# Retention and two MLPs on one core: two rings of PSUM banks, another order of the first units, and the first weights fetched by quarters

## The chip, the core and the metric

The kernel runs on one core of one Trainium2 chip. The metric is the device time of one execution, in microseconds (us). A core has five engines that run side by side, each taking its own instructions in a fixed order: TensorE (PE: matmuls and transposes), VectorE (DVE), ScalarE (ACT), GpSimd (POOL) and SyncE (SP), which here issues nearly all DMAs. They wait for each other through semaphores. TensorE writes its results to PSUM, a small memory of eight banks, from which ACT and DVE fetch them; a bank can be written again only when its readers are done.

## The reference

The inputs are q, k, v of shape (2, 8, 768, 64) (batches, heads, tokens, width), a decay `lam` for each head, and four weight matrices. The first part is retention:

```python
for b in range(nb):                                   # blocks of 64 tokens
    intra = (qb @ kb.T * Dmask) @ vb                  # Dmask[i, j] = lam ** (i - j) where i >= j
    inter = (qb * lam_pow) @ kv_state
    out[:, :, sl] = intra + inter
    kv_state = lam_block * kv_state + (kb * rev_pow).T @ vb
```

Its output, laid out as x of 1536 tokens x 512, goes through two MLPs, each x -> f(x @ w_in) @ w_out with a hidden width of 2048: f is relu squared in the first and max(0.01 h, h) in the second. The weights come as 64-bit floats; the rest is fp32.

## The kernel before

**Retention.** A chunk is 128 tokens (the decay makes the sum independent of the chunk's size). There are 12 units: 2 batches of 6 chunks, each with all 8 heads as 4 pairs. Called `unit n` below, each has these steps:

- `load(n, "kq")`, `load(n, "v")` (L66): 256 KB each, issued by SP into buffers that rotate (five for k, three for q, three for v).
- `transposes(n)` (L279): four transposes of k and four of q on PE, each group into its own PSUM bank; ACT copies them out (L283) as kT and qT. For a chunk with a state before it POOL then scales qT to qS (L289).
- `scores(n)` (L296): the products of kT and qT into two banks, one for the even and one for the odd heads. `mask(n)` (L301): DVE multiplies each bank by the table of decays DTr and writes Pm, which frees the bank.
- `state(n)`: POOL makes kd, the decayed k (L314), and, beyond the first chunk, tmp, the decayed old state (L327). PE multiplies kd with v (L320). DVE writes the new state (L332, or L334 for a batch's first chunk). The last chunk of a batch (units 5 and 11) has none.
- `output(n)`: per pair, state times qS (L345, not for a batch's first chunk, units 0 and 6) and v times Pm (L347). `split` takes the bank away: ACT writes the high part xhi (L69), and after it DVE the low part xlo (L70). xhi and xlo are the MLPs' input.

The order of SP and PE is that of the program; the orders of ACT, DVE and POOL are made by a scheduler, except that steps marked with `keep_in_program_order` keep theirs. `warm` (L205) is PE work without a use, transposes of the identity matrix; there are 15 of them at the start and 7 within `transposes(0)`.

**PSUM.** All tiles of PSUM, in retention and later, come from one pool of eight banks used in turn (`bank`, L59). A new tile takes the bank of the eighth tile before it and waits until that one's readers are done.

**Weights.** A matrix is fetched in pieces of 1 MB (`fetch`, L92; called p0, p1, p2, ... in their order) into two buffers `raw`, each a single DMA: p0 at the loop's i = 1, p1 at i = 9, p2 right after retention. `converting` (L99) turns a piece into fp32 in `hb` and splits it into a high and a low part: ACT L111, four steps of DVE (L112, L113, L115, L118), ACT L132 (w1h or w2h), DVE L134 (w1l or w2l). Each call of `convert` sets off one more of these DVE steps for each piece in work. In retention this happens at i = 3 to 7, so that p0 is whole by the MLPs' first matmul; p1 and p2 are converted at its end and after it. Once the MLPs have begun, the fourth DVE step of a piece, with which its `raw` buffer comes free, also fetches the next piece.

**MLPs.** They need fp32, so each product is three matmuls of high and low parts, all on L525; pairs of token tiles go through a scheme of seven products. Their instructions on PE are in the program's order too. Each of the first steps of the MLPs uses p0 (its low part from the third matmul on), then p1 about 17 us later.

Of the kernel before, what the change touches and what calls it, by code (L numbers as in the profile page):

```python
# [2 lines left out]

# [13 lines left out]
P = 128  # L17
# [3 lines left out]
def tile_retention_then_two_mlps(  # L21
# [32 lines left out]
    raw = ctx.enter_context(tc.tile_pool(name="raw", bufs=2))  # L54
    fp = ctx.enter_context(tc.tile_pool(name="fp", bufs=9))
    cv = ctx.enter_context(tc.tile_pool(name="cv", bufs=1))
    psum = ctx.enter_context(tc.tile_pool(name="psum", bufs=8, space=bass.MemoryType.PSUM))

    def bank():  # L59
        return psum.tile([P, 512], F32, tag="ps", name="ps")  # L60

    def plain():
        return fp.tile([P, TT], F32, tag="f", name="f")
# [1 line left out]
    def dma(dst, src):  # L65
        return nc.sync.dma_start(dst, src)  # L66
# [22 lines left out]
    fetched, at_work = [], []  # L89
    wts, sums, opened = {}, {}, set()  # L90

    def fetch():  # L92
        if todo:
            key = todo.pop(0)
            r = raw.tile([P, 4 * CW], I64, tag="raw", name="raw")
            k = 4 if key[2] == 0 else 2
            dma(r.rearrange("p (k f) -> p k f", k=k), source(*key))
            fetched.append((key, r))

    def converting():  # L100
        key, r = fetched.pop(0)
        l, s, n, h = key
        k = 4 if n == 0 else 2
        words = r.bitcast(U32).rearrange("p (f t) -> p f t", t=2)
        w_lo, w_hi = words[:, :, 0], words[:, :, 1]
        ve = nc.vector
        hb = cv.tile([P, 4 * CW], U32, tag="hb", name="hb", bufs=2)
        hf = hb.bitcast(F32)
        half = hb.bitcast(U16).rearrange("p (f t) -> p f t", t=2)[:, :, 0]

        nc.scalar.activation(hf, w_hi.bitcast(F32), AF.Abs)  # L111
        yield ve.tensor_scalar(out=hf, in0=hf, scalar1=2.0 ** -15, scalar2=122368.0, op0=ALU.max, op1=ALU.min)  # L112
        yield ve.tensor_scalar(out=hb, in0=hb, scalar1=3, scalar2=0x3FFFFFFF,  # L113
                               op0=ALU.logical_shift_left, op1=ALU.bitwise_and)
        yield ve.scalar_tensor_tensor(out=hb, in0=w_hi, scalar=0xC0000000, in1=hb,  # L115
                                      op0=ALU.bitwise_and, op1=ALU.bitwise_or)

        step = ve.scalar_tensor_tensor(out=half, in0=w_lo, scalar=2.0 ** -29, in1=half, op0=ALU.mult, op1=ALU.add)  # L118
        if begun_mlp:
            fetch()  # L120
        yield step
        if (l, s) != stages[0] and n == 0:
            w = hf.rearrange("p (k f) -> p k f", k=k)
            blocks = {(i, j): w[:, 2 * j:2 * j + 2, i * P:(i + 1) * P] for i in range(2) for j in range(2)}
            rb = cv.tile([P, 4 * CW], U32, tag="rb", name="rb")
            yield from weight_sums(key, f"sw{h}", blocks, rb.bitcast(F32))
        while key not in opened:
            yield None
        tags = (f"w1h{h}", f"w1l{h}") if n == 0 else ("w2h", "w2l")
        bufs = 1 if n == 0 else 3  # L130
        hi, lo = (wp.tile([P, 4 * CW], F32R, tag=tag, name=tag, bufs=bufs) for tag in tags)
        nc.scalar.copy(hi, hf)  # L132
        wts[key] = [x.rearrange("p (k f) -> p k f", k=k) for x in (hi, lo)]
        yield ve.tensor_tensor(out=lo, in0=hf, in1=hi, op=ALU.subtract)  # L134
        if (l, s) == stages[-1] and n == 1:
            while ("sums", l, s) not in opened:
                yield None
            rb = cv.tile([P, 4 * CW], U32, tag="rb", name="rb")
            w = hf.rearrange("p (k i m f) -> p k i m f", k=2, i=2, m=2)
            blocks = {(i, j): w[:, j, i] for i in range(2) for j in range(2)}  # L140
            yield from weight_sums(key, f"t{h + 2}", blocks, rb.bitcast(F32))
# [14 lines left out]
                tc.keep_in_program_order(step)  # L156


    begun_mlp = []
    opened.update(order[:5])  # L160

    xhi = [None] * NTILE
# [4 lines left out]
        xlo[t] = xp.tile([P, KD, TT], F32R, tag=f"xlo{t}", name=f"xlo{t}")  # L167

    def retention(ctx_att, att):
        nat = {  # L170
            name: ctx_att.enter_context(tc.tile_pool(name="nat" + name, bufs=n))
            for name, n in (("k", 5), ("q", 3), ("v", 3))
# [25 lines left out]
        make_identity(nc, ident)  # L198


        idle = bank()

        def warm(n):
            for _ in range(n):
                tc.keep_in_program_order(nc.tensor.transpose(idle[:, 0:P], ident, ident))  # L205

# [66 lines left out]
        def transposes(i, names="kq"):  # L273
            for name in names:
                dst = {"k": kT, "q": qT}[name]
                ps = bank().rearrange("p (a s) -> p a s", a=NP)
                src = nats[i, name]
                for p in range(NP):
                    nc.tensor.transpose(ps[:, p, :], src[:, 2 * p:2 * p + 2, :].rearrange("s h d -> s (h d)"), ident)  # L279
                if i == 0:  # L280
                    warm(3 if name == "k" else 4)
                dst[i] = tr.tile([P, NP, C], F32, tag=name, name=name + "T", bufs=2)
                nc.scalar.copy(dst[i], ps)  # L283
            return ps

        def scale_q(i, ps):
            if units[i][1]:
                qS[i] = tr.tile([P, NP, C], F32, tag="qS", name="qS")
                nc.gpsimd.tensor_tensor(out=qS[i], in0=qT[i], in1=LR, op=ALU.mult)  # L289

        def scores(i):
            raw_scores[i] = [bank().rearrange("p (a s) -> p a s", a=NP) for _ in range(2)]
            for p in range(NP):
                for par in range(2):
                    r = slice(par * D, (par + 1) * D)
                    nc.tensor.matmul(raw_scores[i][par][:, p, :], kT[i][r, p, :], qT[i][r, p, :], start=True, stop=True)  # L296

        def mask(i):
            Pm[i] = wk.tile([P, 2, NP, C], F32, tag="Pm", name="Pm")
            for par in range(2):  # L300
                ve.tensor_tensor(out=Pm[i][:, par], in0=raw_scores[i][par], in1=DT[:, par], op=ALU.mult)  # L301
# [65 lines left out]
        scale_q(1, q1)  # L367
        scores(1)
        state(0)
        mask(0)  # L370
        output(0)
        scale_q(2, transposes(2))
        state(1)
        mask(1)
        scores(2)
        for i in range(n_units):
            if i and i + 2 < n_units:
                scale_q(i + 2, transposes(i + 2))
            if i + 4 < n_units:
                load(i + 4, "kq")  # L380
            if i + 2 < n_units:
                load(i + 2, "v")
            if i in (1, 9):
                fetch()
            if i:
                if i > 1:
                    state(i)
                output(i)
                if i + 1 < n_units:
                    mask(i + 1)  # L390
                if i + 2 < n_units:
                    scores(i + 2)
            if 3 <= i <= 7:
                convert(pin=True)


    with ExitStack() as ctx_att:
        att = ctx_att.enter_context(tc.tile_pool(name="att", bufs=1))
        with tc.manual_schedule(engines={mybir.EngineType.SP, mybir.EngineType.PE}):
            retention(ctx_att, att)  # L400


    late = ctx.enter_context(tc.tile_pool(name="late", bufs=1, reuse_waits="tile"))
    spill = [[[dram.tile([P, DM], F32, name=f"spill{l}{t}{m}") for m in range(4)] for t in range(NTILE)]
# [387 lines left out]
            return parts + [first(l, s, 2)] + [second_last(s, t) for t in range(NTILE)]  # L792
        return parts + [second(l, s, 0), first(l, s, 2), second(l, s, 1), second(l, s, 2)]

    begun_mlp.append(True)
    fetch()
    opened.update(order[:7])
    with tc.manual_schedule(engines={mybir.EngineType.PE}):
        for l, s in stages:
# [29 lines left out]
```

## Time and profile before

| | us |
|---|---|
| median of 3 runs (lowest, highest) | 574.09 (573.87, 574.21) |
| the profiled execution | 573.56 |
| its span, from the first instruction to the last | 571.6 |
| PE busy | 561.2 (98% of the span) |
| DVE busy | 407.6 (71%) |
| ACT busy | 304.6 (53%) |
| PE's waits: L525 for DVE g0l L467 | 3.0, 3 times |
| PE's waits: L320, recorded as "issue" | 1.7, once |
| PE's waits: L205 for POOL pw L210 | 1.5, once |
| PE's waits: L296 for ACT qT L283 | 0.8, 3 times |

Retention takes the first 63 us of the span, the MLPs the rest. A row of a timeline gives the start, the length from the first start to the last end of neighbouring instructions of one kind (`x16` is a count in the hardware's records, which is twice the program's for some fp32 matmuls), and in brackets how long the engine had been idle before and what it had waited for. "issue" there stands for a wait that the profile cannot assign to an engine. PEclk is the granted clock of TensorE: 1.00 is 2.4 GHz, 0.50 is 1.2 GHz. A DMA's time to landing runs from its issue to the signal that its data is there.

### The profile page before, as it was taken

Reading aid. Unit: us, or ns where it says so; the run is one execution under the profiler, and the core shown is the slowest. Engines: PE = TensorE matmul, PEld = TensorE weight load, DVE = VectorE, ACT = ScalarE, POOL = GpSimd, SP = SyncE. Lnnn points to the kernel's source line nnn. Section 1 sums busy time; section 2 is a strip of 40 time slices with the busy share of each in tenths; the row PEclk is TensorE's granted clock in tenths of the full one; section 3 lists DMA queues with packets and bytes.
Section 4 is the critical chain, followed back from the end, with each engine's and each line's share of the span. In section 5 each row is a group of like instructions: output and inputs, shape, how many; then the busy total and the mean of one; then the engine's idle time right before and its main releaser. Section 6 shows DMA issues by size and latency. Waiting matters only on the chain.

```text
span 571.6 us, 8193 instructions
## 1 busy us (share of the span) xinstructions
PE 561.2 (98%) x3159; PEld 472.7 (83%) x3159; DVE 407.6 (71%) x595; ACT 304.6 (53%) x486; POOL 89.3 (16%) x101
## 2 busy tenths in 40 slices
PE   7999999999999999999999999999999999999997
PEld 7889888888788878888788888888888888888897
DVE  3588899999745584819888996719663492718887
ACT  2344589553974457733948555543662284435610
POOL 3659100000023202130000000000203101220032
PEclk9999999999999999999999999999999999999999
DMA  8998544535157744294413324354429505560444
GB/s 172 246 209 183 191 147 148 186 146 188 71 73 185 110 148 73 67 202 127 163 32 104 120 73 148 110 185 130 66 43 226 126 4 71 60 87 1 145 151 148
DMA packets 68472, 72.37 MB, mean 127 GB/s; under 512 B 39753, under 2 KB 43857, under 8 KB 68433
## 3 DMA queue, kind: packets, MB, share of 16 engines
q1 hardware_dynamic: 60848, 58.87, 34.2%
q0 software_dynamic: 6912, 12.59, 15.7%
q10 hardware_dynamic: 672, 0.39, 0.3%
q8 instruction: 25, 0.41, 0.3%
q14 instruction: 15, 0.11, 0.1%
HBM read 49.81 MB, written 22.03 MB: 126 GB/s over the span
## 4 chain that ended last, share of the span: by engine, by line
PE 75%; DVE 11%; ACT 6%; DMA 4%; issue 2%; POOL 0%; SPq 0%; ACTq 0%; DVEq 0%; POOLq 0%
PE ps L525 67%; DMA raw<-in_moe_w_in 3%; DVE hb L118 2%; PE ps L279 2%; ACT f L461 2%; PE ps L296 2%; DMA raw<-in_moe_w_out 2%; PE ps L347 1%; DVE hb L115 1%; DVE f L595 1%; ACT g0h L462 1%; PE ps L345 1%; ACT hb L111 1%; ACT f L463 1%; PE ps L320 1%
## 5 line engine op out<-in xcount | busy, mean ns | idle before, releaser
L644 POOL DMA_DIRECT2D spill<-f x48 | 42.7, 918 | 408.3 <-ACT f L640 408.3
L525 PE MATMUL ps<-xhi,w1h 128*128 128x512 f32 x216 | 84.1, 390 | 0.0
L525 PE MATMUL ps<-xhi,w1l 128*128 128x512 f32 x216 | 84.0, 389 | 0.0
L525 PE MATMUL ps<-xlo,w1h 128*128 128x512 f32 x216 | 84.0, 389 | 0.0
L640 ACT COPY f<-ps 128x512 f32<-128x512 f32 x72 | 41.7, 584 | 70.3 <-PE ps L525 69.8
L134 DVE TENSOR_TENSOR w2l<-hb,w2h 128x1024 fp32r<-128x1024 f32 x16 | 19.6, 1227 | 61.1 <-ACT w2h L132 60.7
L467 DVE TENSOR_TENSOR g0l<-f,g0h 128x512 fp32r<-128x512 f32 x52 | 34.7, 686 | 34.2 <-ACT f L463 18.3
L595 DVE TENSOR_TENSOR f<-ps,f 128x512 f32<-128x512 f32 x70 | 45.7, 684 | 9.8 <-PE ps L525 9.3
L525 PEld LDWEIGHTS ps<-xhi,w1h 128*128 128x128 f32 x216 | 40.5, 188 | 8.5 <-issue 0.2
L525 PEld LDWEIGHTS ps<-xhi,w1l 128*128 128x128 f32 x216 | 40.5, 188 | 8.4
L525 PEld LDWEIGHTS ps<-xlo,w1h 128*128 128x128 f32 x216 | 40.5, 188 | 8.4
L525 PE MATMUL ps<-g0l,w2h 128*128 128x512 f32 x112 | 43.9, 392 | 3.0 <-DVE g0l L467 3.0
L111 ACT ACTIVATE hb<-raw 128x1024 f32<-128x1024 f32 x32 | 36.8, 1149 | 14.4 <-DMA raw<-in_moe_w_in 8.7
L118 DVE SCALAR_TENSOR_TENSOR hb<-raw,hb 128x1024 uint16<-128x1024 uint32 x32 | 43.6, 1364 | 0.4
L525 PE MATMUL ps<-g0h,w2l 128*128 128x512 f32 x112 | 43.6, 389 | 0.0
L525 PE MATMUL ps<-g0h,w2h 128*128 128x512 f32 x112 | 43.6, 389 | 0.0
L525 PE MATMUL ps<-t,sw 128*128 128x512 f32 x168 | 40.4, 389 | 0.0
L525 PE MATMUL ps<-w2l,g0h 128*128 128x512 f32 (+1 forms) x104 | 39.6, 381 | 0.0
L525 PE MATMUL ps<-w2h,g0l 128*128 128x512 f32 (+1 forms) x104 | 39.6, 381 | 0.0
L525 PE MATMUL ps<-w2h,g0h 128*128 128x512 f32 (+1 forms) x104 | 39.6, 381 | 0.0
L115 DVE SCALAR_TENSOR_TENSOR hb<-raw,hb 128x1024 uint32<-128x1024 uint32 x32 | 39.1, 1221 | 0.4
L525 PEld LDWEIGHTS ps<-t,sw 128*128 128x128 f32 x168 | 31.5, 188 | 6.5
(186 smaller groups left out, 1238.3 us busy)
## 6 DMA issues: line engine op xcount, KB each, us to landing
raw<-in_moe_w_in SPq DMA_DIRECT2D x16, 1024.0 KB, 5.7
raw<-in_moe_w_out SPq DMA_DIRECT2D x16, 1024.0 KB, 4.9
spill<-f POOLq DMA_DIRECT2D x48, 256.0 KB, 4.6
spill<-f SPq DMA_DIRECT2D x24, 256.0 KB, 3.1
k<-in_k SPq DMA_DIRECT2D x12, 256.0 KB, 4.7
q<-in_q SPq DMA_DIRECT2D x12, 256.0 KB, 5.0
v<-in_v SPq DMA_DIRECT2D x12, 256.0 KB, 5.3
f<-spill SPq DMA_DIRECT2D x12, 256.0 KB, 2.6
```

The costliest lines, as they stand in the source:

```text
L111: nc.scalar.activation(hf, w_hi.bitcast(F32), AF.Abs)
L115: yield ve.scalar_tensor_tensor(out=hb, in0=w_hi, scalar=0xC0000000, in1=hb, op0=ALU.bitwise_and, op1=ALU.bitwise_or)
L118: step = ve.scalar_tensor_tensor(out=half, in0=w_lo, scalar=2.0 ** -29, in1=half, op0=ALU.mult, op1=ALU.add)
L134: yield ve.tensor_tensor(out=lo, in0=hf, in1=hi, op=ALU.subtract)
L279: nc.tensor.transpose(ps[:, p, :], src[:, 2 * p:2 * p + 2, :].rearrange("s h d -> s (h d)"), ident)
L296: nc.tensor.matmul(raw_scores[i][par][:, p, :], kT[i][r, p, :], qT[i][r, p, :], start=True, stop=True)
L461: nc.scalar.activation(r, src, AF.Relu)
L467: nc.vector.tensor_tensor(out=glo, in0=r, in1=ghi, op=ALU.subtract)
L525: nc.tensor.matmul(ps, a, b, start=start and n == 0, stop=stop and n == len(ops) - 1, skip_group_check=again)
L595: ve.tensor_tensor(out=out, in0=ps[h, where], in1=other, op=ALU.add)
L640: nc.scalar.copy(f, src)
L644: nc.gpsimd.dma_start(dst, f, accum_op=ALU.add)
```

## The change

- PSUM in retention is a pool `early` with two rings of four banks: `ps` for transposes, tables, states, outputs and warm, and `scores` for the scores. A new tile takes the bank of the fourth tile before it in its own ring. The MLPs have a pool of eight banks of their own, opened after retention. Each call of `warm` takes a bank of its own.
- In the first units PE gets nine more transposes of the identity and `transposes(2)` between `state(0)` and `output(0)`; `transposes(3)` and `state(2)` stand after `output(1)`, where `transposes(3)` stood ahead of `output(1)` and `state(2)` behind `transposes(4)`.
- p0 and p1 are fetched by quarters of 256 KB, one in each of the loop's steps i = 1 to 8, behind that step's loads of k, q and v. p2 is fetched at i = 9. The conversion's `fetch` holds for every piece but p0.
- The DVE steps of p0's conversion are set off at i = 6 to 11.

```diff
-    psum = ctx.enter_context(tc.tile_pool(name="psum", bufs=8, space=bass.MemoryType.PSUM))
-    def bank():
-        return psum.tile([P, 512], F32, tag="ps", name="ps")
+    banks = []
+    def bank(tag="ps"):
+        return banks[-1].tile([P, 512], F32, tag=tag, name="ps")
...
+    def fetch_by_rows():
+        key = todo.pop(0)
+        r = raw.tile([P, 4 * CW], I64, tag="raw", name="raw")
+        fetched.append((key, r))
+        for k in range(4):
+            dma(r.rearrange("p (k f) -> p k f", k=4)[:, k], source(*key)[:, k])
+            yield
...
         step = ve.scalar_tensor_tensor(out=half, in0=w_lo, scalar=2.0 ** -29, in1=half, op0=ALU.mult, op1=ALU.add)
-        if begun_mlp:
+        if key != order[0]:
             fetch()
...
     def retention(ctx_att, att):
+        banks.append(ctx_att.enter_context(tc.tile_pool(name="early", bufs=4, space=bass.MemoryType.PSUM)))
...
-        idle = bank()
         def warm(n):
+            idle = bank()
             for _ in range(n):
                 tc.keep_in_program_order(nc.tensor.transpose(idle[:, 0:P], ident, ident))
...
         def scores(i):
-            raw_scores[i] = [bank().rearrange("p (a s) -> p a s", a=NP) for _ in range(2)]
+            raw_scores[i] = [bank("scores").rearrange("p (a s) -> p a s", a=NP) for _ in range(2)]
...
         scores(1)
         state(0)
+        warm(9)
+        q2 = transposes(2)
         mask(0)
         output(0)
-        scale_q(2, transposes(2))
+        scale_q(2, q2)
         state(1)
         mask(1)
         scores(2)
+        pieces = chain(fetch_by_rows(), fetch_by_rows())
         for i in range(n_units):
-            if i and i + 2 < n_units:
+            if i > 1 and i + 2 < n_units:
                 scale_q(i + 2, transposes(i + 2))
             if i + 4 < n_units:
                 load(i + 4, "kq")
             if i + 2 < n_units:
                 load(i + 2, "v")
-            if i in (1, 9):
+            if 1 <= i <= 8:
+                next(pieces)
+            if i == 9:
                 fetch()
             if i:
-                if i > 1:
+                if i > 2:
                     state(i)
                 output(i)
+                if i == 1:
+                    scale_q(3, transposes(3))
+                    state(2)
                 if i + 1 < n_units:
                     mask(i + 1)
                 if i + 2 < n_units:
                     scores(i + 2)
-            if 3 <= i <= 7:
+            if 6 <= i:
                 convert(pin=True)
...
+    banks.append(ctx.enter_context(
+        tc.tile_pool(name="psum", bufs=8, space=bass.MemoryType.PSUM, reuse_waits="tile")))
...
-    begun_mlp.append(True)
-    fetch()
     opened.update(order[:7])
```

TensorE from scores(1) on. Before: the rows are scores(1), state(0), output(0), transposes(2), state(1), scores(2), transposes(3) and the first of output(1).

```order
L296 MATMUL ps<-qT,kT 128x128 x8
L320 MATMUL ps<-v,kd 64x64 x8
L347 MATMUL ps<-Pm,v 64x128 x8
L279 MATMUL ps<-ident,k 128x128 x4
L279 MATMUL ps<-ident,q 128x128 x4
L320 MATMUL ps<-v,kd 64x64 x8
L296 MATMUL ps<-qT,kT 128x128 x8
L279 MATMUL ps<-ident,k 128x128 x4
L279 MATMUL ps<-ident,q 128x128 x4
L345 MATMUL ps<-qS,st_170 64x128 x2
```

The same place on TensorE after the change, from scores(1) to the first of output(1); L303 are scores, L327 states, L354 and L352 outputs.

```order
L303 MATMUL ps<-qT,kT 128x128 x8
L327 MATMUL ps<-v,kd 64x64 x8
L212 MATMUL ps<-ident 128x128 x9
L286 MATMUL ps<-ident,k 128x128 x4
L286 MATMUL ps<-ident,q 128x128 x4
L354 MATMUL ps<-Pm,v 64x128 x8
L327 MATMUL ps<-v,kd 64x64 x8
L303 MATMUL ps<-qT,kT 128x128 x8
L352 MATMUL ps<-qS,st_170 64x128 x2
```

Nine transposes of the identity and those of unit 2 now stand ahead of output(0), and output(1) follows scores(2) at once.

ScalarE at the end of retention, from the copy of unit 11's qT to the first eviction of the MLPs. Before: xhi of units 9, 10 and 11 with L111 of p1 and of p2 between them.

```order
L283 COPY qT<-ps 128x512
L69 CAST xhi_843<-ps 128x4x128
L111 ACTIVATE hb<-raw 128x1024
L69 CAST xhi_843<-ps 128x4x128
L111 ACTIVATE hb<-raw 128x1024
L69 CAST xhi_843<-ps 128x4x128
L461 ACTIVATE f<-ps 128x512
```

The same place on ScalarE after the change; L119 is the first step of p1 and then of p2, and w1h_982 is the high part of p0.

```order
L290 COPY qT<-ps 128x512
L119 ACTIVATE hb<-raw 128x1024
L140 CAST w1h_982<-hb 128x1024
L69 CAST xhi_857<-ps 128x4x128 x2
L119 ACTIVATE hb<-raw 128x1024
L69 CAST xhi_857<-ps 128x4x128
L477 ACTIVATE f<-ps 128x512
```

The first step of p1 and the high part of p0 now stand ahead of unit 9's xhi.

VectorE at the end of retention, from Pm of unit 10 to xlo of unit 10. Before:

```order
L301 TENSOR_TENSOR Pm<-ps,DTr 128x512 x2
L332 TENSOR_TENSOR st_168<-ps,tmp 64x4x64 x2
L70 TENSOR_TENSOR xlo_844<-ps,xhi_843 128x4x128
L301 TENSOR_TENSOR Pm<-ps,DTr 128x512 x2
L332 TENSOR_TENSOR st_170<-ps,tmp 64x4x64 x2
L112 TENSOR_SCALAR hb<-hb 128x1024
L113 TENSOR_SCALAR hb<-hb 128x1024
L70 TENSOR_TENSOR xlo_844<-ps,xhi_843 128x4x128
```

The same place on VectorE after the change; L126 is the fourth step of p0 and L142 its low part.

```order
L308 TENSOR_TENSOR Pm<-ps,DTr 128x512 x2
L126 SCALAR_TENSOR_TENSOR hb<-raw,hb 128x1024
L339 TENSOR_TENSOR st_168<-ps,tmp 64x4x64 x2
L70 TENSOR_TENSOR xlo_858<-ps,xhi_857 128x4x128
L308 TENSOR_TENSOR Pm<-ps,DTr 128x512 x2
L339 TENSOR_TENSOR st_170<-ps,tmp 64x4x64 x2
L142 TENSOR_TENSOR w1l_983<-hb,w1h_982 128x1024
L70 TENSOR_TENSOR xlo_858<-ps,xhi_857 128x4x128
```

The fourth step of p0 now stands ahead of unit 9's state, and its low part stands where the first two steps of p1 stood.

## Rows read from the trace of the kernel before

**Rows 1.** The page, slices of the span: granted TensorE clock in tenths.

```profile
PEclk9999999999999999999999999999999999999999
```

**Rows 2.** Waits of TensorE over the whole span: us, times, longest.

```profile
PE ps L525 <- DVE g0l L467: 3.0, 3, 1.0
```

**Rows 3.** TensorE's timeline, 8 to 21 us: start, us, instruction, [idle before].

```profile
13.94 1.12 PE L320 MATMUL ps<-v,kd 128*64 128x64 f32 x16 [1.70 <-issue]
```

**Rows 4.** VectorE's timeline, 10 to 18 us.

```profile
13.15 2.48 DVE L301 TENSOR_TENSOR Pm<-ps,DTr 128x512 f32<-128x512 f32 x4 [6.72 <-DMA DTr<-tab]
```

**Rows 5.** GpSimd's timeline, 9 to 18 us.

```profile
10.83 2.04 POOL L314 TENSOR_TENSOR kd<-k,kdec 128x512 f32<-128x512 f32 x2 [7.90 <-ACT kdec L265]
```

**Rows 6.** Windows: length, busy us by engine, PEclk, DMA share, GB/s.

```profile
13.70:17.10 3.40, 3.16 (x34) 2.86 (x35) 2.69 (x6) 0.29 (x1) 2.21 (x4) 0.50 1.10 205
17.10:20.50 3.40, 3.23 (x46) 2.81 (x45) 2.09 (x4) 1.37 (x3) 2.17 (x3) 1.00 0.94 211
25.00:28.00 3.00, 3.00 (x60) 2.83 (x62) 1.25 (x4) 1.27 (x3) 2.34 (x3) 1.00 1.04 344
```

**Rows 7.** Four DMA issues of SyncE, each with its time to landing.

```profile
L66 SPq DMA_DIRECT2D v<-in_v x1: 368/368/368, 6.9 to 6.9; - x1
...
DMA to landing us min/median/max: 2.9/2.9/2.9
...
L66 SPq DMA_DIRECT2D q<-in_q x1: 726/726/726, 8.8 to 8.8; - x1
...
DMA to landing us min/median/max: 6.8/6.8/6.8
...
L66 SPq DMA_DIRECT2D k<-in_k x1: 972/972/972, 19.0 to 19.0; - x1
...
DMA to landing us min/median/max: 4.6/4.6/4.6
...
L66 SPq DMA_DIRECT2D v<-in_v x1: 402/402/402, 48.9 to 48.9; - x1
...
DMA to landing us min/median/max: 4.8/4.8/4.8
```

**Rows 8.** TensorE's timeline, 21 to 37 us.

```profile
22.77 1.16 PE L296 MATMUL ps<-qT,kT 64*128 64x128 f32 x16
...
27.25 1.16 PE L296 MATMUL ps<-qT,kT 64*128 64x128 f32 x16
28.34 0.66 PE L279 MATMUL ps<-ident,k 128*128 128x128 f32 x4
...
29.36 0.69 PE L320 MATMUL ps<-v,kd 128*64 128x64 f32 x16
29.88 0.39 PE L345 MATMUL ps<-qS,st 128*64 128x128 f32 x4
...
32.21 1.16 PE L296 MATMUL ps<-qT,kT 64*128 64x128 f32 x16 [0.41 <-ACT qT L283]
```

**Rows 9.** ScalarE's timeline, 29 to 34 us.

```profile
30.03 1.18 ACT L111 ACTIVATE hb<-raw 128x1024 f32<-128x1024 f32 x1 [2.08 <-DMA raw<-in_moe_w_in]
```

**Rows 10.** VectorE's timeline, 53 to 64 us.

```profile
54.61 1.28 DVE L301 TENSOR_TENSOR Pm<-ps,DTr 128x512 f32<-128x512 f32 x2
...
58.48 0.69 DVE L70 TENSOR_TENSOR xlo<-ps,xhi 128x512 fp32r<-128x512 f32 x1 [1.42 <-ACT xhi L69]
...
60.28 0.87 DVE L332 TENSOR_TENSOR st<-ps,tmp 64x256 f32<-64x256 f32 x2
```

**Rows 11.** The page, costliest groups: busy, mean ns.

```profile
L118 DVE SCALAR_TENSOR_TENSOR hb<-raw,hb 128x1024 uint16<-128x1024 uint32 x32 | 43.6, 1364 | 0.4
```

**Rows 12.** Groups of ScalarE's instructions by line, 0 to 66 us.

```profile
L132 ACT CAST w1h<-hb 128x1024 fp32r<-128x1024 f32 x1 | 1.0, 1046 | 1.0 <-DVE hb L118 1.0
```

**Rows 13.** ScalarE's timeline, 53 to 66 us.

```profile
55.59 0.59 ACT L283 COPY qT<-ps 128x512 f32<-128x512 f32 x1
57.86 0.58 ACT L69 CAST xhi<-ps 128x512 fp32r<-128x512 f32 x1 [1.68 <-PE ps L347]
```

More of the change, by code (lines that the diff above doesn't have):

```diff
@@ L1 @@
 from contextlib import ExitStack
-from itertools import islice
+from itertools import chain
 import concourse.bass as bass
@@ L156, in convert @@
                 tc.keep_in_program_order(step)
-    begun_mlp = []
     opened.update(order[:5])
```

## The prediction

> **What bounds the kernel now.** I read the page first, for what is busiest: TensorE, 98% of the span by the table, and its granted clock is full in every slice [rows 1]. So only TensorE's idle time, half-clock time and useless work can be won. Its waits over the whole span come next: 7.0 us in all. The largest group, three waits of about 1 us for g0l, lies in the MLPs [rows 2], and nothing in the change touches what PE waits for there. The rest of this comparison is therefore retention's first 63 us. Third, the timelines of that stretch, for who is late at each wait; last, the DMA issues, since the reader will see that the loads, not the banks, are late next.
>
> **The start, part by part.** PE has ended scores(1) at 13.94 - 1.70 = 12.24 and idles until state(0) at 13.94 [rows 3]. What ends that wait is a bank: the tile of state(0) takes the bank of the even scores of unit 0, which DVE reads until the first half of L301 is done, some 0.65 us after 13.15; and L301 starts that late because of the table DTr [rows 4]. Two separate rings take this wait away. The next conditions are already met: the first of GpSimd's two kd ends near 10.83 + 1.02 = 11.85 [rows 5], and v of unit 0 landed at 6.9 + 2.9 = 9.8 [rows 7]. After the idle, the granted clock was at its lower level (0.50, 1.2 GHz) from 13.7 to 17.1 and at the upper (2.4 GHz) again from 17.1 [rows 6].
>
> Prices at full clock come from unit 4: scores 28.34 - 27.25 = 1.09, eight transposes 29.36 - 28.34 = 1.02, state 29.88 - 29.36 = 0.52; a unit without a wait takes 27.25 - 22.77 = 4.48, which leaves 1.85 for the output [rows 8]. An output without a state has half the matmuls: 0.93. A transpose is 1.02 / 8 = 0.13, so the nine added ones cost 1.15, all of it on PE.
>
> The new order, run with these prices from 12.24:
> - state(0) to 12.76, nine transposes to 13.91.
> - transposes(2) now stand ahead of output(0) and need k and q of unit 2. q lands at 8.8 + 6.8 = 15.6 [rows 7]; before, the idle time and the half clock hid that. k has no landing on record; it is ahead of q in the queue, and its four transposes (0.51) fit in front of q. So q's four run from 15.6 to 16.1: 1.2 us of new idle, in two pieces.
> - output(0) to 17.05, state(1) to 17.57, scores(2) to 18.66, output(1) to 20.51, transposes(3) to 21.53.
> - state(2), moved ahead of scores(3), needs v of unit 2. Its landing is not on record, but it is just ahead of k of unit 5, which lands at 19.0 + 4.6 = 23.6, and a 256 KB load at 211 GB/s takes 1.24 [rows 6, 7]. I take 22.36; bounds are 21.5 (no wait) and 23.6. So state(2) runs to 22.9, after 0.8 us of idle, and scores(3) starts at 22.9 against 22.77 before [rows 8].
> - From there unit 2's state is behind it: scores(4) at 22.9 + 4.48 - 0.52 = 26.86 against 27.25, a lead of 0.4 (by the bounds of v, 1.2 and -0.85).
>
> So what looks like 1.7 us of wait and 3.4 us of half clock removed comes back as 1.15 of useless transposes and about 2.0 of waiting for q and v. If the half clock appears here again, PE has the 0.8 before v to lose it in.
>
> **ACT in mid-retention.** scores(5) waited 0.41 for qT [rows 8], because L111 of the first piece, held until its data came, kept ACT until 30.03 + 1.18 = 31.2, just ahead of the copies [rows 9]. That conversion now starts at i = 6, when its quarters are long there. 32.21 - 27.25 - 4.48 = 0.48 is gained, so scores(5) is 0.9 ahead. The four DVE steps move too; a unit's own DVE work with one of them is 1.28 + 0.87 + 0.69 + 1.36 = 4.20 [rows 10, 11], still under 4.48, so I price that at nothing.
>
> **The tail of retention.** Here the deferred conversion comes due. DVE's fourth step of p0 (1.36) [rows 11] stands between Pm of unit 10, which ended at 54.61 + 1.28 = 55.89, and unit 9's state: it ends at 57.25. ACT's w1h needs it and takes 1.05 [rows 12]: 58.30. xhi of unit 9 stands behind w1h, and before it started at 57.86, straight after output(9) [rows 13]: 0.44 late against PE. Behind it DVE is packed (xlo, Pm, state, from 58.48 to 61.15) [rows 10], and output(11), which started at 61.1, needs that last state. So the 0.44 passes to the end of retention: 0.9 - 0.44 is a lead of 0.46.
>
> Ahead of w1h on ACT is the first step of p1, which needs all four quarters of p1, and the last is issued right behind v of unit 10. That v landed at 48.9 + 4.8 = 53.7 [rows 7]. A quarter takes 0.76 at the 344 GB/s seen while a piece came in [rows 6]. The four of p1 are 3.05 us that the queue did not carry so early before. If the queue's idle moments absorb the other three, the last lands at 54.5; if none is absorbed, at 56.75. ACT is free for it at 56.18 [rows 13] less the lead, 55.3. With 1.18 for L111 [rows 9] and 1.05 for w1h, xhi would start at 57.55 (early quarter) to 59.0 (late), against 57.86: -0.3 to +1.1 at the end of retention. The same queue brings v of units 7 to 9 later, by up to the three earlier quarters, 2.3; that can only eat the lead. With the quarter half-way, at 55.6, and half of the lead of 0.9 eaten, DVE's step is the later gate: 0.44 - 0.45 = 0.0; with all of it eaten, +0.44. I take +0.3, nearer to the second, because loads of 256 KB were already held to 211 GB/s with the queue full [rows 6].
>
> The Trainium skill, in DMA: Bandwidth & Descriptors, section Bandwidth, tells to batch DMAs to 1 MiB or more, which speaks against quarters. No run so far shows a quarter; the full piece came in at 344 GB/s [rows 6]. By the page the four quarters would take longer than the piece, and the late end above, 1.1, would be the likelier one; by the row it would not.
>
> **After retention.** Conversions of p1 and p2 on DVE end about 2 us later against PE's start; w1l of p1 is needed only some 17 us after their start. I price it at nothing; if that cover is gone, PE waits up to 1.5.
>
> **The sum.** 573.56 + 0.3 = 573.9 for an execution like the profiled one. That execution was 0.53 below the median of the runs shown, so 574.4 as a time to be measured.
>
> **Rivals.**
> - A, the lead survives: the queue absorbs the quarters, and retention ends 0.3 to 0.5 early. For it: the queue does carry 344 GB/s with large rows [rows 6]. Against it: the L126 gate stays. 573.6.
> - B, the start gives what its waits suggest: q and v of unit 2 come early enough, so that 2.0 of idle falls away. For it: v's landing is not on record. Against: q's is, and SP's order ahead of it is unchanged. About -1.6: 572.5.
> - C, slower: ACT stands before the last quarter. Place: L119 of p1, ahead of w1h and unit 9's xhi. It decides from a landing past 56. At 57 xhi starts at 59.25, 1.4 late, and PE then idles 1.4 between output(10) and output(11); an idle of 1.7 was followed by 3.4 us at half clock [rows 3, 6], that is 1.7 lost at the most. 1.4 + 0.9 (half of it, the idle being shorter): 576.4.
> - D, slower, DVE's backlog shows in the MLPs: +1.5, 575.6.
> - E, the clock falls in the start: two idles near 0.6. The waits of 1.0 in the MLPs left the clock full [rows 1, 2], the 1.7 did not. At most 1.7 lost, of which v's wait covers 0.8: 575.3. The Trainium skill, in TensorE: Matmul & The Clock Gate, section A second HAM failure mode: psum-queue depth-cycling, says that short idles between groups of matmuls can make the clock go back and forth; by that rule E is the outcome, and the rows on the MLPs' waits speak against it here.
>
> **Chances.** The forecast 0.47 (own range 573.6 to 575.4), A 0.18, B 0.13, C 0.12, D 0.05, E 0.05. A measurement of this kernel tells 0.2%, 1.15 us, from no change. Faster by more than that: B and a part of A, 0.17. Slower: C, half of D and E, and the forecast's upper end, 0.25. Same: 0.58. The range, 572.4 to 576.4, reaches from B to C and takes in the bounds of v and of the quarter.
>
> **What would show it.** Right: no idle ahead of state(0), full clock from 13.7 to 17.1, idles ahead of q's transposes near 15 and ahead of state(2) near 22, scores(4) near 26.9, no idle ahead of scores(5) from ACT; at the end xhi of unit 9 starting behind w1h, not behind output(9), and the first L541 within 0.5 us of its place before, near 63. Wrong: the last quarter landing past 56.5, a PEclk under 1 anywhere after 10 us, or PE waiting in the MLPs anywhere but for g0l.

## The result, and the profile after

The changed kernel takes 577.5 us (median of 4 runs, 577.31 to 577.94) against 574.15 (573.87 to 574.57) for the kernel before in the same session: a ratio of 1.0059, 95% interval 1.0043 to 1.0075, so 3.4 us slower. The forecast was 574.4, its range ended at 576.4. The profiled execution has a span of 575.5 us, 3.9 more than the profiled one of before.

TensorE's waits over the whole span, as in [rows 2] (us, times, longest); of 7 groups the start's own wait for pw, the same as before, is left out:

```profile
PE ps L541 <- DVE g0l L483: 3.6, 4, 1.3
PE ps L354 <- DVE xlo L70: 2.8, 1, 2.8
...
PE ps L327 <- DMA v<-in_v: 0.8, 1, 0.8
PE ps L286 <- DMA k<-in_k: 0.5, 1, 0.5
PE ps L286 <- DMA q<-in_q: 0.5, 1, 0.5
PE ps L303 <- ACT qT L290: 0.2, 1, 0.2
```

The waits for k, q and v are the start's. One wait of 2.8 us is new and one of those for g0l is added. The start first, TensorE's timeline from 11.5 to 18 us, against [rows 3, 8]:

```profile
11.97 0.69 PE L327 MATMUL ps<-v,kd 128*64 128x64 f32 x16
12.59 1.20 PE L212 MATMUL ps<-ident 128*128 128x128 f32 x9
14.32 0.63 PE L286 MATMUL ps<-ident,k 128*128 128x128 f32 x4 [0.54 <-DMA k<-in_k]
15.40 0.63 PE L286 MATMUL ps<-ident,q 128*128 128x128 f32 x4 [0.45 <-DMA q<-in_q]
15.96 1.09 PE L354 MATMUL ps<-Pm,v 128*64 128x128 f32 x16
```

The idle time of 1.70 ahead of state(0) is gone, and the window that was at half clock in [rows 6] now has it in full:

```profile
13.70:17.10 3.40, 2.41 (x33) 1.98 (x34) 2.46 (x5) 1.17 (x2) 2.46 (x4) 1.00 1.04 209
```

Then v of unit 2 is waited for (0.78, state(2) at 22.32), scores(4) starts at 26.94 (27.25 before), and scores(6) at 35.91 against 36.69: a lead of 0.78. It ends in the middle of retention. TensorE from 42 to 46 us:

```profile
42.03 0.69 PE L327 MATMUL ps<-v,kd 128*64 128x64 f32 x16
45.54 0.66 PE L354 MATMUL ps<-Pm,v 128*64 128x128 f32 x8 [2.82 <-DVE xlo L70]
```

Follow that wait backwards. It names VectorE, whose timeline says that it was itself idle:

```profile
44.79 0.69 DVE L70 TENSOR_TENSOR xlo<-ps,xhi 128x512 fp32r<-128x512 f32 x1 [6.27 <-ACT xhi L69]
```

ScalarE, 36 to 64 us, shows why unit 5's xhi came so late: the first conversion step of p0 stands ahead of it and waits 4.35 for its data. The last four rows are the tail of retention, which answers to [rows 13]:

```profile
38.23 0.59 ACT L290 COPY qT<-ps 128x512 f32<-128x512 f32 x1
43.17 1.12 ACT L119 ACTIVATE hb<-raw 128x1024 f32<-128x1024 f32 x1 [4.35 <-DMA raw<-in_moe_w_in]
44.20 0.56 ACT L69 CAST xhi<-ps 128x512 fp32r<-128x512 f32 x1
...
57.99 0.59 ACT L290 COPY qT<-ps 128x512 f32<-128x512 f32 x1
58.47 1.19 ACT L119 ACTIVATE hb<-raw 128x1024 f32<-128x1024 f32 x1
59.61 1.04 ACT L140 CAST w1h<-hb 128x1024 fp32r<-128x1024 f32 x1
60.56 0.58 ACT L69 CAST xhi<-ps 128x512 fp32r<-128x512 f32 x1
```

And SyncE issued the last quarter of p0, the one of loop step i = 4, only here:

```profile
37.10 0.79 SPq L66 DMA_DIRECT2D raw<-in_moe_w_in  x1
```

The trace has no landing of it; L119's wait ended 6.1 us after the issue. scores(8) starts 2.26 late, where scores(7) had been 0.78 early: 3.04 lost. At the end of retention ScalarE is late once more: p1's last quarter, issued at 53.77, landed at 57.6, and xhi of unit 9 started at 60.56, 2.7 later than in [rows 13], where TensorE was already 2.41 late (scores(11) at 60.15 against 57.74). The 0.3 between the two comes back in output(11), which takes 2.28 instead of 2.00. The MLPs start at 65.79, against 63.10: +2.69. A second loss of 1.05 follows in the MLPs, between 148 and 155 us, where before there was one wait of 0.94 (at 150.25):

```profile
150.92 0.50 PE L541 MATMUL ps<-g0l,w2h 128*128 128x512 f32 x1 [0.27 <-DVE g0l L483]
...
154.00 0.50 PE L541 MATMUL ps<-g0l,w2h 128*128 128x512 f32 x1 [1.27 <-DVE g0l L483]
```

From there to the end the distance is constant, +3.8.

### The profile page after: what moved, and what is told of

The parts are those of the page before. It is cut to its first block, busy times and chain, and to the rows that moved or that the text cites. A ratio compares the mean times of both kernels' runs of the same rounds, so it can differ in the third digit from the quotient of the medians.

```text
span 575.5 us, 8231 instructions
## 1 busy us (share of the span) xinstructions
PE 562.1 (98%) x3168; PEld 472.4 (82%) x3168; DVE 406.7 (71%) x595; ACT 304.0 (53%) x486; POOL 88.5 (15%) x101
## 4 chain that ended last, share of the span: by engine, by line
PE 72%; DVE 12%; ACT 7%; DMA 6%; issue 2%; SPq 0%; ACTq 0%; DVEq 0%
PE ps L541 67%; DMA raw<-in_moe_w_in 2%; DVE hb L126 2%; DMA raw<-in_moe_w_out 2%; ACT f L477 2%; DVE hb L123 2%; ACT hb L119 1%; PE ps L303 1%; DVE f L611 1%; PE ps L354 1%; DMA q<-in_q 1%; PE ps L286 1%; ACT g0h L478 1%; ACT f L479 1%; DVE hb L120 1%
## 5 line engine op out<-in xcount | busy, mean ns | idle before, releaser
L142 DVE TENSOR_TENSOR w2l<-hb,w2h 128x1024 fp32r<-128x1024 f32 x16 | 19.5, 1226 | 60.2 <-ACT w2h L140 59.9
L119 ACT ACTIVATE hb<-raw 128x1024 f32<-128x1024 f32 x32 | 36.7, 1147 | 16.6 <-DMA raw<-in_moe_w_in 7.9
L126 DVE SCALAR_TENSOR_TENSOR hb<-raw,hb 128x1024 uint16<-128x1024 uint32 x32 | 43.9, 1371 | 0.4
```

## The experiments

"Shift" below is the start of the MLPs' first matmul, and then of their last ones, against the kernel before (63.10 and 565.83), each from one profiled execution. Such executions differ from the first units on: scores(0) starts at 7.81 in the kernel before, at 6.91 in run 9, whose start is the same, and from 6.90 to 7.94 in all, so a few tenths of a shift tell little. Ratios go with the runs of the kernel before in the same session (medians 573.9 to 574.3). The changed kernel has three parts: banks and start (rings, nine transposes, new order of the first units, a PSUM pool of its own for the MLPs), first pieces by quarters, and conversion from i = 6 on.

**1. The first step behind unit 6's xhi.** ScalarE's L119 of p0 keeps the place in which the program names it.

```
-        nc.scalar.activation(hf, w_hi.bitcast(F32), AF.Abs)
+        hold = tc.keep_in_program_order if key == order[0] else (lambda step: step)
+        hold(nc.scalar.activation(hf, w_hi.bitcast(F32), AF.Abs))
```

> Theory (late quarter): ScalarE's first step of p0 stood ahead of unit 5's xhi and was held until p0's last quarter landed, and output(6) waited for that bank. Here only that one instruction is kept behind unit 6's xhi, where the quarter (about 43) is there. The idle of 2.8 ahead of output(6) goes, scores(8) starts near 43.5 instead of 46.6, and the time is 577.5 - 3.0 = 574.5. The conversion stays late, so the second loss, about 1.05 at the end of the first paired block (150 us), stays. Rival (a ring of four banks is too short by itself): output(6) still waits for xlo of unit 5 by 1 us or more, 576 to 577.

577.67 us, ratio 1.0058 (1.0043 to 1.0073): missed, nothing gained. The wait of 2.8 is gone, so its cause is shown; but TensorE waits 2.06 ahead of output(11), at 63.20, behind this on ScalarE:

```profile
58.32 1.16 ACT L120 ACTIVATE hb<-raw 128x1024 f32<-128x1024 f32 x1 [2.59 <-DMA raw<-in_moe_w_in]
59.38 1.04 ACT L141 CAST w1h<-hb 128x1024 fp32r<-128x1024 f32 x1
60.31 0.59 ACT L69 CAST xhi<-ps 128x512 fp32r<-128x512 f32 x1
```

The second late quarter, p1's, had been hidden behind the first. TensorE is 0.45 early at scores(11) and 2.45 late at the MLPs, so the tail costs 2.9, of which the profile names 2.06 as a wait. Shift +2.45, at the end +4.74.

**2. One ring of eight in retention.** The wait was in a bank of the ring of four, so the ring might have been to blame.

```
-        ... tc.tile_pool(name="early", bufs=4, ...)
+        ... tc.tile_pool(name="early", bufs=8, ...)
-            raw_scores[i] = [bank("scores")...
+            raw_scores[i] = [bank()...
```

> Only the two rings of four are undone: one ring of eight banks in retention, all else as changed. Theory (late quarter): output(6) does not wait, but scores(8) does, for kT and qT of unit 8, which stand behind the held instruction on ScalarE: it starts near 45.8 instead of 46.6. The start loses some 0.6 by the bank of state(0). Together 577.0 to 577.5. Rival (ring too short): the wait goes, 574.5.

577.67, ratio 1.0052 (1.0036 to 1.0069), from the timed runs alone; no profile of this run is read. The time is near the theory's and not the rival's, but run 1 has the same time without the wait, so this run alone does not clear the ring. Runs 1 and 3 do: both keep the rings of four, and output(6) does not wait. That kT and qT of unit 8 were held here, behind the same L119, is argued and not shown.

**3. The quarters of p0 two at a time, at i = 1 and 2.**

```
-            if 1 <= i <= 8:
+            for _ in range({1: 2, 2: 2, 5: 1, 6: 1, 7: 1, 8: 1}.get(i, 0)):
                 next(pieces)
```

> p0's four quarters in the steps i = 1 and 2 (two each) instead of 1 to 4; p1's as changed. Theory (late quarter): the last quarter is issued near 26 and lands by 32, ScalarE is not held, the idle of 2.8 goes: 574.5, with the loss of about 1.05 at 150 us still there. Rival (small transfers cost the queue itself): a wait of the same size comes in mid-retention for v or for the same instruction, 576 or more.

576.86, ratio 1.0042 (1.0027 to 1.0057): missed. The 2.8 is gone here too, by an earlier landing and not by another order on ScalarE, and again the tail takes over (1.44, at 62.63):

```profile
57.76 1.16 ACT L119 ACTIVATE hb<-raw 128x1024 f32<-128x1024 f32 x1 [1.66 <-DMA raw<-in_moe_w_in]
```

Shift +1.88, at the end +3.86.

**4. Whole pieces.** Banks, start and late conversion stay; each piece is one load again, and fetched where it was before.

```
-            if 1 <= i <= 8:
-                next(pieces)
-            if i == 9:
+            if i in (1, 9):
                 fetch()
```

> p0 and p1 by one DMA each at i = 1 and 9, p2 after retention, as before; banks, start and late conversion as changed. Theory: the piece lands at 30 and ScalarE's first step stands ahead of unit 5's copies, so the start's lead is lost there (scores(5) near 32.2), no 2.8 idle; late conversion costs 0.4 at retention's end and about 1.05 at 150 us: 575.4. Rival (the late conversion costs nothing, all of the loss is the quarter): 574.1.

575.2, ratio 1.0019 (1.001 to 1.0029), as expected. Shift +0.08, so the quarters are what retention lost by. At the end +1.66: the MLPs lose 1.6 without any quarter.

**5. Banks and start alone** (the edit of run 4, and `3 <= i <= 7` again).

> Banks and start as changed; pieces whole and the conversion at i = 3 to 7 as before. Theory: the start is worth 0.4 at scores(4), but ScalarE's first step of p0 stands ahead of unit 5's copies and waits for the piece near 30, so scores(5) starts near 32.0 and the lead left is 0.2; no wait in mid-retention, nothing lost in the MLPs. 573.9 to 574.3 beside a before of 574.28, no change that can be told. Rival (the two rings of four or the new start themselves cost time): 575 or more.

575.26, ratio 1.0027 (1.0016 to 1.0038): missed. The shift, -0.18, was as expected, but the end is at +1.96. A wait that no kernel so far had stands in the MLPs' first stage, on TensorE:

```profile
99.16 0.50 PE L539 MATMUL ps<-t,w2h 128*128 128x512 f32 x1 [1.04 <-DVE t L481]
```

VectorE there: the last low part of t stands behind L120, L121 and L442:

```profile
95.35 0.69 DVE L481 TENSOR_TENSOR t<-f,t 128x512 fp32r<-128x512 f32 x1
95.96 0.68 DVE L120 TENSOR_SCALAR hb<-hb 128x1024 f32<-128x1024 f32 x1
96.68 0.69 DVE L121 TENSOR_SCALAR hb<-hb 128x1024 uint32<-128x1024 uint32 x1
97.29 1.22 DVE L442 TENSOR_TENSOR sw<-rb,sw 128x1024 fp32r<-128x1024 f32 x1
98.42 0.69 DVE L481 TENSOR_TENSOR t<-f,t 128x512 fp32r<-128x512 f32 x1
```

In the kernel before it is done ahead of them; this is its VectorE:

```profile
95.74 0.69 DVE L467 TENSOR_TENSOR t<-f,t 128x512 fp32r<-128x512 f32 x1
96.35 0.69 DVE L112 TENSOR_SCALAR hb<-hb 128x1024 f32<-128x1024 f32 x1
97.07 0.69 DVE L113 TENSOR_SCALAR hb<-hb 128x1024 uint32<-128x1024 uint32 x1
97.68 1.22 DVE L428 TENSOR_TENSOR sw<-rb,sw 128x1024 fp32r<-128x1024 f32 x1
```

**6. Late conversion alone.** The kernel before with one condition changed.

```
-            if 3 <= i <= 7:
+            if 6 <= i:
                 convert(pin=True)
```

> The kernel before with one edit: p0's DVE steps at i = 6 to 11 instead of 3 to 7. Theory (backlog): retention ends within 0.5 of 63.1, DVE enters the MLPs with three or more steps of 0.7 to 1.3 more to do, has no idle time to take them up until 146, and PE waits longer for g0l at 150: +1.4, so 575.7. Rival (the loss in the MLPs comes with the new pool of banks): no change, 574.3.

575.08, ratio 1.0021 (1.0011 to 1.0032). Shift +0.58, and +1.78 at the end. The tail is what the prediction described, on ScalarE:

```profile
57.50 1.04 ACT L132 CAST w1h<-hb 128x1024 fp32r<-128x1024 f32 x1 [1.01 <-DVE hb L118]
58.45 0.58 ACT L69 CAST xhi<-ps 128x512 fp32r<-128x512 f32 x1
```

xhi of unit 9 starts at 58.45, not 57.86. Of these 0.59, TensorE was late by 0.31 already: scores(5) waited for qT, as ScalarE began on the piece at 30.31, not 30.03 [rows 9]. The gate's own part is 0.28, which output(11) loses; the prediction had 0.44. The other 1.2 is lost near 150 us, for g0l.

**7. The edit of run 1 on the kernel of run 5.**

> e5 with one edit more: ScalarE's first step of p0 kept in program order, which puts it behind unit 3's xhi instead of ahead of unit 5's copies. Theory: the piece is there by then, no wait of ScalarE ahead of scores(5), the lead of 0.8 to 0.9 is kept to the MLPs: 573.4 to 573.6, a little faster than before. Rival (a later gate takes the lead, as at the tail of e1): 574.2.

575.59, ratio 1.0026 (1.0013 to 1.0038): missed, as run 5. No profile of it is read.

**8. Run 5 without the nine transposes** (`warm(9)` taken out).

> e5 without the nine added transposes of the identity. PE idles from the end of state(0), about 12.5, until k of unit 2 lands, about 14.3. Theory (an idle like the 1.7 of before lets the clock fall): granted clock near 0.5 for some 3 us after, 1.5 us lost there, of which the wait for v at 22 covers 0.8; 0.3 to 0.7 above e5. Rival (the nine are useless): clock stays at 1, same as e5.

575.53, ratio 1.0035 (1.0021 to 1.0049), near run 5's. (The profiled execution, 577.88, had a wait of 2.3 behind a late piece at 34 us and half clock for 3.4 us after it; neither is part of the edit.) TensorE idled 1.50 ahead of k's transposes instead, and the clock did not fall behind that idle:

```profile
14.20:17.10 2.90, 2.32 (x34) 1.95 (x36) 1.80 (x4) 1.20 (x3) 2.34 (x4) 1.00 1.20 211
```

So the nine neither cost nor gave anything that this run can tell.

**9. The new PSUM pool alone.** The kernel before, one ring of eight in retention and a second pool of eight for the MLPs.

```
+        banks.append(ctx_att.enter_context(tc.tile_pool(name="early", bufs=8, ...)))
...
+    banks.append(ctx.enter_context(tc.tile_pool(name="psum", bufs=8, ..., reuse_waits="tile")))
```

> The kernel before with one edit: retention and the MLPs get a pool of eight banks each, as the change opens one for the MLPs; no rings, old start, whole pieces, early conversion. The scheduler then orders VectorE in the first stage of the MLPs otherwise: the last t low part stands behind three more conversion steps. Theory (order): retention unchanged, PE waits 0.8 to 1.0 for t at 99, about 0.4 more by 155: 575.3. Rival (e5's loss came from the rings or the start): no change, 574.0.

575.06, ratio 1.0019 (1.001 to 1.0029). Shift +0.02, end +1.74, with the wait of 1.09 for t at 99.43. So this edit alone makes the difference of run 5; it has two parts, the second pool and its `reuse_waits="tile"`, which are not told apart. The run also shows what a better start can give here. TensorE idled 1.85 ahead of state(0), as in the old order, but the clock stayed at 1.00, and scores(4) came 1.10 earlier than in the kernel before (0.90 of it stood at scores(0) already). Yet scores(5) started at 32.23 against 32.21, because ScalarE began on the piece of p0 only at 30.06 (30.03 in [rows 9]): this landing takes back any lead ahead of it.

**10. Both rings in one pool.** Run 5, but one pool of two rings of four, which the MLPs take by turns; the order on VectorE in the MLPs is then that of the kernel before.

```
+    psum = ctx.enter_context(tc.tile_pool(name="psum", bufs=4, ...))
+    turn = []
     def bank(tag="ps"):
-        return banks[-1].tile(...)
+        if turn:
+            turn.append(0)
+            tag = ("ps", "scores")[len(turn) % 2]
+        return psum.tile(...)
```

> e5 with the banks from one pool throughout: two rings of four, from which the MLPs take banks by turns. The scheduler's order in the MLPs is then that of before, and the instructions of retention are those of e5. Theory (order): no wait at 99, the MLPs take as long as before, the lead of 0.2 at their start stays: 573.8 to 574.0, against e5's 575.3. Rival: same as e5.

574.04, ratio 0.9999 (0.999 to 1.0008): 1.2 less than run 5, and level with the kernel before. Shift +0.21, at the end +0.35. So the rings, the nine and the new start, by themselves, are worth nothing either way.

**11. Run 10 with the edit of run 1.**

> e10 with ScalarE's first step of p0 kept in program order, behind unit 3's xhi. Theory: it does not wait there, no idle ahead of scores(5), the lead of 0.8 stays to the end: 573.2 to 573.4, faster than before by 0.1%. Rival (a later gate takes it): 573.9.

573.87, ratio 0.9995 (0.9986 to 1.0004): not shown to be faster. The profiled execution (574.56) is the slowest of the eleven: shift -0.10, a wait of 1.27 for g0l at 150.73 (before: 0.94 at 150.25), and +1.20 at the end. It does not show what the other executions made of the lead.

**12. Run 11 with p1 by quarters, at i = 5 to 8.**

> e11 with p1 alone by quarters, at i = 5 to 8 as in the change. Theory: its last quarter lands near 57.6, ScalarE's first step of p1 stands ahead of unit 9's xhi and holds it to 58.8, output(11) waits for the last state, and retention ends 1.3 to 1.9 later than in e11; 575.0 to 575.5. Rival (the conversion's lateness, not the quarter, made the tail late): as e11.

575.75, ratio 1.0033 (1.002 to 1.0046). The size was as expected, the mechanism was not: p1's last quarter landed at 55.63, early enough for ScalarE; its three steps on VectorE then stood ahead of unit 9's xlo and the last state, and output(11) waited for st and for Pm:

```profile
61.53 0.89 PE L357 MATMUL ps<-qS,st 128*64 128x128 f32 x4 [0.73 <-DVE st L344]
62.71 0.43 PE L359 MATMUL ps<-Pm,v 128*64 128x128 f32 x2 [0.29 <-DVE Pm L313]
63.07 0.50 PE L545 MATMUL ps<-xhi,w1h 128*128 128x512 f32 x1
63.50 0.32 PE L359 MATMUL ps<-Pm,v 128*64 128x128 f32 x1
...
65.18 0.50 PE L545 MATMUL ps<-xlo,w1h 128*128 128x512 f32 x1
```

The first matmul of the MLPs has a shift of -0.03, but its row stands in the middle of output(11), whose matmuls go on behind it. The second, at 65.18, was at 63.43 before. So retention ended 1.75 late, and the MLPs lost only 0.1 more (+1.86 at the end). Quarters of p1 alone, with p0 whole and converted early, make the tail late.

**13. The changed kernel with the first steps of both pieces behind** (the edit of run 1 with `key in order[:2]`; p1's then stands behind the last xhi).

> The changed kernel with ScalarE's first step of both quartered pieces (L119 of p0 and p1) kept in the order in which the program names it, so that p1's stands behind the last xhi of retention and not ahead of unit 9's. Theory (each late quarter gates retention once, through the place of its L119 on ScalarE; the second is hidden behind the first): no wait of TensorE ahead of output(6) and none ahead of output(11), the MLPs start 0.5 to 0 us before their place in the kernel before; the MLPs lose 1.2 to 1.7 from the new PSUM pool and the late conversions, so 574.6 to 575.6. Rival (the loading of the queue by the quarters itself costs retention its end, through v and q of the last units): a wait of 1 to 2 us stays in the last three units, MLPs start 1.5 to 2 late, 577.

576.56, ratio 1.0045 (1.003 to 1.006). The theory missed; the rival's figures came near (a wait of 1.08, shift +1.66), but not by its mechanism. There is no wait ahead of output(6), p1's L120 is gone from the tail, and a wait stays ahead of output(11), for the last state and not for a load:

```profile
62.40 0.78 PE L353 MATMUL ps<-qS,st 128*64 128x128 f32 x3 [1.08 <-DVE st L340]
```

ScalarE now waits for VectorE, with no load in between:

```profile
58.58 1.04 ACT L141 CAST w1h<-hb 128x1024 fp32r<-128x1024 f32 x1 [2.65 <-DVE hb L127]
59.53 0.58 ACT L69 CAST xhi<-ps 128x512 fp32r<-128x512 f32 x1
```

That is the prediction's own gate, p0's fourth step, but the step took 2.31 instead of 1.36:

```profile
56.23 2.31 DVE L127 SCALAR_TENSOR_TENSOR hb<-raw,hb 128x1024 uint16<-128x1024 uint32 x1
```

GpSimd had started just ahead of it:

```profile
56.09 1.27 POOL L297 TENSOR_TENSOR qS<-qT,LR 128x512 f32<-128x512 f32 x1
```

TensorE was 0.25 early at scores(11), so this tail costs 1.9. Shift +1.66, end +3.74. So three gates follow one another, each hidden while the one before it stands: p0's last quarter in mid-retention, then p1's last quarter and p0's fourth step at the tail.

**14. Run 13 in one pool**, as in run 10.

> The kernel of the run before with the PSUM banks of both rings in one pool whose two tags the MLPs take by turns. Theory (the new pool costs 1.2 to 1.7 in the MLPs by another order of VectorE's steps): 1 to 1.5 faster than the run before, 573.6 to 574.4, level with the kernel before. Rival (what the MLPs lose there comes from the later conversions of p1 and p2 alone): within 0.3 of the run before.

576.81, ratio 1.0045 (1.0029 to 1.0062), within 0.3 of run 13: the rival held. With the conversions late, the MLPs lose as much (+2.1 in the profile) in the one pool as in the new one. The two losses of the MLPs, by the pool (runs 5 and 9) and by the late conversion (runs 6 and 14), don't add; either is enough.

## Why the prediction was wrong

- **The start: right, in part by luck.** State(0) without a wait, full clock, waits for q and v where forecast (0.45 for q and 0.78 for v; k's own 0.54 and q's make 1.0 against 1.2), scores(4) at 26.94 (26.86). But 0.20 of the 0.31 won there stood already at scores(0) (7.61 against 7.81), ahead of the parts that the sum priced. The sum gave the start a lead of 0.4, to be eaten at the tail; runs 5 and 10 show no gain that can be told, and run 9 that the landing of the whole p0 takes back such a lead at scores(5). Rival B is out. So is E: the clock stayed at 1.00 behind all these idles. The rule that E leaned on, in the Trainium skill, TensorE: Matmul & The Clock Gate, section A second HAM failure mode: psum-queue depth-cycling, did not show in this trace.
- **ScalarE in mid-retention: this step failed.** "That conversion now starts at i = 6, when its quarters are long there." I took the loop step in which a quarter is issued for its time. SyncE came to the step i = 4 at 37.10, with full queues ahead, and the quarter was there near 43.1; ScalarE, where L119 is not tied to i = 6 and stood ahead of unit 5's xhi, waited 4.35. What was priced as a gain (the wait for qT gone: lead 0.78, forecast 0.9) became a loss of 3.04. Runs 1 and 3 show it from two sides, since either another place on ScalarE or an earlier load takes the 2.8 away. It is the mechanism of my rival C, on the other piece: C looked at p1 alone, and priced the wait at 1.4 and the clock at 0.9; behind the wait of 2.82 the clock stayed at 1.00.
- **The tail: the kind right, the sizes wrong.** The last quarter of p1 landed at 57.6, past the forecast's 54.5 to 56.75; my own bound for "wrong" was 56.5. It is hidden in the changed kernel, whose TensorE was late already, and comes out in runs 1 and 3, whose tails, from scores(11) to the MLPs, cost 2.9 and 2.0. The gate by p0's fourth step cost 0.28 in run 6 (0.44 forecast) and 1.9 in run 13. The forecast priced that step at the mean of 1.36, whatever GpSimd was doing then; behind a step of GpSimd it took 2.31.
- **The queue.** The forecast let idle moments of the queue absorb the quarters, each at 0.76 by the 344 GB/s of [rows 6]. That rate is of all transfers in that window together; in the kernel before, p0 itself, 1 MB, took 8.0 us from its issue at 22.00 to its landing. In the changed kernel a quarter, a fourth of that, took 3.8 to 6.1, and SyncE, with the loads of k, q and v between them, came to p0's last quarter 15.3 us after its first (21.79 and 37.10). The Trainium skill, in DMA: Bandwidth & Descriptors, section Bandwidth, advises large batches; these rows go its way. Run 4, with whole pieces, starts the MLPs at +0.08.
- **After retention: this step failed too.** Conversions that end later were priced at nothing (rival D, 0.05, had 1.5). Run 6 shows 1.2 for them alone. With it falls what the prediction said of the waits for g0l at its start, that nothing in the change touches what PE waits for there. And I did not see that a new PSUM pool for the MLPs changes the order in which VectorE's work there is put: 1.7 in run 9, whose only edit it is.
- **The sum.** In the profile: -0.78 at 40 us, 3.04 lost at output(6), 0.43 more up to the MLPs (no wait above 0.1 in it; output(11) alone takes 2.28, from 63.51 to 65.79, against 2.00), 1.05 at 150 us and 0.09 later: +3.8. By its place the last 1.1 is the late conversion's: it lies at 148 to 150 us, as all of that loss does in run 6 and 1.8 of 2.1 in run 14, and not at 99, where the new pool alone loses most (runs 5 and 9). Its size stays open: late conversion alone cost 1.2 in run 6 and 2.1 in run 14, both edits together 1.1 here and 1.6 to 2.3 in runs 1, 3, 4 and 13.

## What to carry to other kernels

When a load is cut into pieces that are issued in different loop steps, take the landing of the last piece from the time at which the issuing engine gets to it in the trace, and then ask what stands behind its first reader on that reader's engine. Removing one late gate tells little while others lie 1 or 2 us behind it: here it took three edits to see them all, and a kernel without any of them (run 10) only came back to the time of before. A wait further on can also take back a lead, if what it waits for does not come earlier with TensorE: in run 9 a lead of 1.10 at scores(4) was gone at scores(5), behind a load that landed when it did before. And steps that are moved to a later place need idle time there: VectorE is busy 44.4 of the 46 us from 100 to 146 in the kernel before, and in run 6 the loss by the steps put off stands right behind that stretch, at 148 to 150.

## What the runs showed of the hardware

On the steps below, VectorE and GpSimd held each other up. In run 13 GpSimd's L297 started at 56.09 and ended at 57.36; L127 on VectorE, started at 56.23, took 2.31, 0.95 more than its mean of 1.36 [rows 11]. In the changed kernel the order was the other way round: VectorE started first and kept its time, and GpSimd's step took 1.95 in place of 1.27. VectorE of the changed kernel:

```profile
58.21 1.37 DVE L126 SCALAR_TENSOR_TENSOR hb<-raw,hb 128x1024 uint16<-128x1024 uint32 x1
```

and its GpSimd:

```profile
58.73 1.95 POOL L296 TENSOR_TENSOR qS<-qT,LR 128x512 f32<-128x512 f32 x1 [0.38 <-ACT qT L290]
```

The later of the two is longer by about what the first still had to go (0.95 longer with 1.13 to go in run 13, 0.68 with 0.85 here). The Trainium skill, in SBUF — State Buffer, section SBUF: two separate sides, calls the port that the two engines share an exclusive lock for a whole instruction; the rows agree with it. Not every pair meets like this: in the changed kernel GpSimd's L334 (from 57.03) and VectorE's L308 (from 57.01) ran side by side, and two of each took 1.31 and 1.28, as they do alone.

An idle time of about 1.5 us in the start was followed by half clock in one kernel and not in another. In run 6 (1.53 us idle up to 13.64) this window followed:

```profile
13.70:15.50 1.80, 1.80 (x26) 1.80 (x28) 1.80 (x4) 0.00 (x0) 0.86 (x2) 0.50 1.23 218
```

In run 8, idle 1.50 up to 14.17, it stayed at 1.00, and so it did in run 9, idle 1.85 up to 13.19:

```profile
13.70:17.10 3.40, 3.11 (x52) 2.67 (x49) 2.79 (x6) 1.66 (x3) 2.28 (x3) 1.00 1.35 222
```

Later in run 8 an idle of 2.26 up to 33.96 was followed by 0.50 (33.8 to 37.2), and in the changed kernel one of 2.82 up to 45.54 by 1.00. So the length of the idle alone does not tell what the clock does; what does was not tried.
